# A planner's rule in a transformer block: LayerNorm of blocks 2 to 5 is taken first

## The chip, the cores and the metric

The kernel runs on one core of one Trainium2 chip. The core has a matrix engine (TensorE, PE in the profile), a vector engine (VectorE, DVE), an activation engine (ScalarE, ACT), a general engine (GpSimd, POOL) and a sequencer that issues transfers (SyncE, SP). Each engine executes its own stream of instructions in order and waits on semaphores for the others. The metric is the device time of one execution in microseconds (us).

## The reference

One transformer block on 2048 tokens of width 640, in float32. Attention has 32 heads of 20 columns and a sliding window of 256 keys; the feed-forward part is gated, 1536 wide.

```python
x = A_x                                               # [1, 2048, 640]
qkv = layernorm(x) @ wqkv                             # q, k, v: 32 heads of 20
scores = einsum("bhqd,bhkd->bhqk", q, k) * 20 ** -0.5
mask = (i - j >= 0) & (i - j < 256)                   # query i, key j
p = softmax(where(mask, scores, -1e9))
h = x + (p @ v) @ wo
g = layernorm(h)
out = h + (gelu(g @ w_gate) * (g @ w_up)) @ w_down
```

LayerNorm has no weights: (x - mean) / sqrt(var + 1e-5) over the 640 columns of a token.

## The kernel before, in words

The tokens are cut into 16 blocks of 128 (a block is one tile of 128 partitions), and two blocks make a chunk for the projections of q and k. A float32 product is made of three float16 products, so each operand is split into a high part and a low part: `xh`, `xl` for the normalised input, `w0h`, `w0l` (q), `w1h`, `w1l` (k), `w2h`, `w2l` (v), `w3h`, `w3l` (output projection) for the weights. ScalarE makes a high part, and VectorE makes the low part with one SCALAR_TENSOR_TENSOR of 128x640 (method `low`, L442).

The way of a block through the first half is this. `load_x` (L713) fetches it. `x_lane` (L673) runs `layernorm` (L467): two BN_STATS and one BN_AGGR on VectorE, an addition there, a power on GpSimd (tile `ly` with the lane's letter: `lyxc` for block 2, `lyxd` for block 3, `lyx` for block 4 and later), three small operations on VectorE, and one TENSOR_SCALAR of 128x640 that writes the normalised block in place (`pt` for blocks 1 to 3, `xt` for the others). Blocks 0 to 3 are then transposed on TensorE (`transpose_part`, L522): ScalarE copies the high part out, VectorE subtracts for the low part. Blocks 4 and later are split first (tile `xp`) and transposed by two DMAs on SP's queue (`turned`, L505). Then `qk` (L721) multiplies a chunk into bank `mm` on TensorE, in three groups of two, two and one tile of columns. `qk_out` (L746) takes a group out in tile `qks` (ScalarE the high part, VectorE the low part) and ScalarE's queue writes it to memory, from where `stack` (L767) fetches it back as `qT` and `kT` with six DMAs each on SP's queue. `vproj` makes v of a block in 30 matmuls.

Attention needs each row's maximum ahead of the exponentials. `maxima` (L833) multiplies q and k in bank `ra` or `rb` (matmuls `<-kT,qT`, 60 rows), and `max_out` (L905) reduces them on VectorE into `mxs` (CUSTOM_DVE into `junk`, then a read of the accumulator). When a block has all 32, `max_transpose` (L935) turns them on TensorE (tile `m`, then `mT`) and two DMAs of ScalarE's queue put them into two further rows of `qT`. `scores` (L950) multiplies again with these rows (matmuls `<-qT,kT`, 62 rows), ScalarE takes the exponential into `pt`, GpSimd masks it, and `value_lane` (L1015) multiplies with v into bank `pv`. The output projection and the whole feed-forward part follow; the first products of the latter fill TensorE while attention still runs.

What sets the order of all this is a planner inside the kernel. Class `Clock` (L54) keeps a modelled time for each engine. The program's pieces are generators ("lanes"), and each names the engine and the tiles that its next instruction needs. The main loop at the end of `block_kernel` goes through a list of lanes and lets the first that can start issue its next instruction; where none can, the modelled time goes on by 0.03 us. So a lane's place in the list and the lead that it is granted (variable `back`: how far ahead of the present its engine may already be planned) set the order of each engine's stream. Built once, the order is fixed. The list at L1636 is: lanes that must go soon, the list `early`, `outs` (results taken out of a bank: `qk_out`, `max_out`, the weights' `low`), `trans` (transposes), the other `sides`, and attention and dense products last. `early` holds every `x_lane` while the planner's condition at L1624 holds.

One more rule concerns TensorE. While no scores have been planned and TensorE has nothing to do by the plan, the loop issues a matmul that nothing reads, from the identity into bank `pv`; the text calls these fillers:

```python
if not pos["score"] and nc.t["tensor"] <= now:
    nc.tensor.matmul(pv[:, 0, :], ident16, ident16, start=True, stop=True)
```

They stand in TensorE's stream like any other matmul, and are executed there whether or not TensorE would have had to wait.

Of the kernel before, what the change touches and what calls it, by code (L numbers as in the profile page):

```python
# [253 lines left out]
def block_kernel(ctx: ExitStack, tc: tile.TileContext, x, wqkv, wo, wg, wu, wd, out):  # L254
# [44 lines left out]
    OUT, PREP, RAMPMAX, FFPREP, LATE = 0.75, 0.55, 0.25, 0.2, 0.4  # L299
    LEAD, TARGET = 20, 0.0  # L300
    XF = 1
    FFBACK = dict(split_lane=0.4, scale_lane=0.4, chunk_lane=0.3, token_sums=0.1,
                  sums_lane=0.2, norm_lane=0.2)
    EARLY = 0.6
# [234 lines left out]
    def products(n, term, ready=None, at_=None):  # L539


        ps = [at_[0]] if at_ else []
        col = at_[1] if at_ else 0

        def start(i):
            if ready and not ready(i) or not ps and opened["mm"] >= banks["mm"]:
                return INF
            t = nc.ready([x for ab in term(i) for x in ab], "tensor")
            return t if ps else max(t, nc.slot(psums["mm"], "mm", banks["mm"]))

        for i in range(n):
            yield ("tensor",), lambda i=i: start(i)
            if not ps:
                ps.append(bank("mm"))
            m = term(i)
            for k, (l, r) in enumerate(m):
                if k:
                    yield pe()
                o = ps[0][:, col:col + r.free_size()]
                nc.tensor.matmul(o, l, r, start=(i == 0 and k == 0),  # L560
                                 stop=(i == n - 1 and k == len(m) - 1))
                pos["dense"] += r.free_size() * 3 // len(m)
        return o
# [102 lines left out]
    B = [Block() for _ in range(NB)]  # L666
# [891 lines left out]
    class Lane:  # L1558
# [11 lines left out]
        def start(self, now):  # L1570

            if "tensor" in self.engs:
                return nc.t["tensor"] <= now + AHEAD and self.need() <= max(now, nc.t["tensor"])
            name = self.gen.__name__
            back = self.back
            if name in ("split_lane", "scale_lane"):
                back = PREP if not W["o", 0].ready else FFPREP
            elif name == "x_lane":
                back = EARLY if not B[XF].full else LATE
            elif name == "max_out" and not W["v"].ready:  # L1580
                back = RAMPMAX
            if isinstance(self.engs, Soon):
                back = max(back, OUT)
            if ffpools[1]:
                back = FFBACK.get(name, OUT)
            return (all(nc.t[e] <= now + back for e in self.engs if e != "sync")
                    and self.need() <= now + 0.1)
# [18 lines left out]
    sides, trans, outs = [], [], []  # L1606
# [7 lines left out]
    while dense.alive or sides or side or outs or tasks:  # L1614
        while side:
            back, gen = side.pop(0)
            sides.append(Lane(gen, back))
        while tps:
            trans.append(Lane(tps.pop(0), OUT))
        while tasks:  # L1620
            outs.append(Lane(tasks.pop(0), OUT))
        att_lanes = [rows, values]
        ahead = pos["dense"] / DENSE - pos["score"] / (H // 2) - TARGET
        early = [l for l in sides if l.gen.__name__ == "x_lane"] if not B[XF].full else []  # L1624
        if not W["v"].ready:
            att_first = maxq or nc.t["vector"] < nc.t["tensor"]
        else:
            att_first = ahead > 0
        if W["o", 0].ready:
            outs.sort(key=lambda l: l.gen.__name__ == "low")  # L1630
        if nc.mode == "row":
            early = [values] + early
        elif len(valq) < 2 and (maxq or scoreq):
            att_lanes = [rows]
        first = [l for l in [values] + trans + sides if isinstance(l.engs, Soon)]
        order = (first + early + outs + trans + sides  # L1636
                 + (att_lanes + [dense] if att_first else [dense] + att_lanes))
        for lane in order:
            if lane.alive and lane.start(now):
                break  # L1640
        else:
            if not pos["score"] and nc.t["tensor"] <= now:
                nc.tensor.matmul(pv[:, 0, :], ident16, ident16, start=True, stop=True)
            now += 0.03
            idle += 1
            assert idle < 20001, "nothing can be issued"
            continue
        idle = 0
        lane.step()
        trans = [l for l in trans if l.alive]  # L1650
        outs = [l for l in outs if l.alive]
        sides = [l for l in sides if l.alive]
# [44 lines left out]
```

## Time and profile before

| | us |
|---|---|
| median of 3 runs | 1022.67 (1022.4 to 1022.76) |
| the profiled execution, its own time | 1023.17 |
| its span, first to last instruction | 1021.3 |
| TensorE busy in the span | 999.8 |
| VectorE, ScalarE, GpSimd busy | 754.8, 437.0, 298.0 |

The profile comes from one execution, whose time is 0.5 us above the median; 1.9 us of it lie outside the span. In the rows of the timeline the first number is the start in us from the beginning of the span, the second the duration of the group, then engine, line, operation, output<-input, shapes and count; in brackets stands the idle time of the engine just ahead of it and who ended it. Almost all instructions are recorded under line L199, the line of a helper, so the tiles tell them apart. A matmul is shown with its whole passage through the array, so that rows of successive matmuls overlap: what one costs in a row of many is the distance between two starts.

### The profile page before, as it was taken

What the parts mean: (1) busy time and instruction counts of PE and PEld (TensorE: products, weight loads), DVE (VectorE), ACT (ScalarE), POOL (GpSimd) and SP (SyncE); (2) the same over time, 40 slices, a digit from 0 to 9 for tenths busy, and PEclk for the clock granted to TensorE, in tenths of its full rate; (3) what the DMA queues carried; (4) which work ended last, traced back from release to release, by engine and by line L of the source; (5) the groups of instructions that cost most, each with busy time, mean ns of one, the idle gap of its engine ahead of it and who ended that gap; (6) DMA issues with size and microseconds to landing.
All of it is one profiled execution on the core that took longest, in us unless ns stands there. A gap on an engine that the chain in (4) does not pass through costs nothing.

```text
span 1021.3 us, 30777 instructions
## 1 busy us (share of the span) xinstructions
PE 999.8 (98%) x12921; PEld 695.8 (68%) x12921; DVE 754.8 (74%) x2221; ACT 437.0 (43%) x706; POOL 298.0 (29%) x489
## 2 busy tenths in 40 slices
PE   8999999999999999999999999999999999999998
PEld 7875666676666676776655564567777777777776
DVE  6888998986787787474788788798996975544553
ACT  6514654656555564654558543522222222221220
POOL 7102223443343342342436321255313310000000
PEclk9999999999999999999999999999999999999999
DMA  8657667361551524225033433223553532222211
GB/s 306 137 116 175 184 145 168 81 163 55 91 122 44 114 57 118 42 61 127 3 131 106 92 117 103 78 104 127 161 177 90 161 138 78 78 96 86 78 53 52
DMA packets 105835, 112.67 MB, mean 110 GB/s; under 512 B 38369, under 2 KB 79585, under 8 KB 105697
## 3 DMA queue, kind: packets, MB, share of 16 engines
q1 hardware_dynamic: 93600, 99.97, 35.9%
q10 hardware_dynamic: 12096, 10.75, 3.4%
q8 instruction: 101, 1.65, 0.7%
q14 instruction: 38, 0.30, 0.1%
HBM read 73.73 MB, written 28.84 MB: 100 GB/s over the span
## 4 chain that ended last, share of the span: by engine, by line
PE 82%; DVE 8%; DMA 4%; ACT 2%; issue 2%; SPq 1%; POOL 0%; ACTq 0%; DVEq 0%
PE mm L199 41%; PE pv L199 12%; PE ra L199 11%; PE rb L199 10%; PE tp L199 7%; DVE junk L199 2%; DVE am L199 1%; DVE ht L199 1%; DMA v<-in_wqkv_dram 1%; DMA gu<-in_wqkv_dram 1%; SPq L199 1%; DMA qT<-mT 1%; DVE m L199 1%; ACT pt L199 1%; DMA h_dram<-ht 1%
## 5 line engine op out<-in xcount | busy, mean ns | idle before, releaser
L199 POOL TENSOR_SCALAR_AFFINE_SELECT pt<-pt 128x512 f32<-128x512 f32 x352 | 175.3, 513 | 278.2 <-ACT pt L199 262.6
L199 DVE CUSTOM_DVE_ANT_0 junk<-rb,band 128x320 bf16<-128x320 f32 x230 | 112.5, 489 | 41.3 <-PE rb L199 35.9
L199 DVE CUSTOM_DVE_ANT_0 junk<-ra,band 128x320 bf16<-128x320 f32 x218 | 106.6, 489 | 43.8 <-PE ra L199 38.3
L199 ACT ACTIVATE pt<-ra,esc 128x640 f32<-128x640 f32 (+2 forms) x131 | 99.6, 767 | 66.2 <-PE ra L199 53.3
L199 ACT ACTIVATE pt<-rb,esc 128x640 f32<-128x640 f32 (+2 forms) x125 | 94.9, 766 | 77.2 <-PE rb L199 56.5
L199 PE MATMUL pv<-pt,v 128*21 128x128 f32 x2880 | 104.1, 275 | 1.1 <-ACT oT L199 1.1
L199 PEld LDWEIGHTS <-ah 128*128 128x128 f16 x768 | 75.0, 98 | 29.5 <-issue 2.1
L199 ACT ACTIVATE gel<-gel,ffk 128x512 f32<-128x512 f32 x36 | 26.0, 721 | 138.0 <-DVE gel L199 138.0
L199 PEld LDWEIGHTS pv<-pt,v 128*21 128x21 f32 x2880 | 68.6, 100 | 11.9 <-issue 2.1
L199 PEld LDWEIGHTS <-ws 128*128 128x128 f16 x720 | 70.3, 98 | 8.3
L199 PEld LDWEIGHTS <-kT 62*64 62x64 f16 x2880 | 61.9, 107 | 13.9 <-issue 10.1
L199 PEld LDWEIGHTS <-qT 60*64 60x64 f16 x1280 | 29.8, 104 | 60.3 <-issue 51.3
L199 PEld LDWEIGHTS <-gu 128*128 128x128 f16 x440 | 42.1, 98 | 36.1 <-issue 2.5
L199 DVE SCALAR_TENSOR_TENSOR ht<-mm,ffk,ht 128x320 f32<-128x320 f32 x96 | 52.1, 545 | 10.9 <-PE mm L199 9.0
L199 ACT CAST ah<-gel 128x512 f16<-128x512 f32 x48 | 29.6, 617 | 64.4 <-DVE gel L199 64.2
L199 PE MATMUL mm<-xh,w1h 128*128 128x256 f16 x200 | 54.7, 274 | 1.3 <-DVE qks L199 1.3
L199 PE MATMUL mm<-xl,w1h 128*128 128x256 f16 x200 | 54.7, 273 | 0.0
L199 PE MATMUL mm<-xh,w1l 128*128 128x256 f16 x200 | 54.7, 273 | 0.0
L199 PE MATMUL mm<-w3l,oh 128*128 128x320 f16 x160 | 48.1, 301 | 0.1
L199 PE MATMUL mm<-w2h,xh 128*128 128x320 f16 x160 | 48.1, 300 | 0.0
L199 PE MATMUL mm<-w2h,xl 128*128 128x320 f16 x160 | 48.1, 301 | 0.0
L199 PE MATMUL mm<-w3h,ol 128*128 128x320 f16 x160 | 48.1, 300 | 0.0
(299 smaller groups left out, 2521.3 us busy)
## 6 DMA issues: line engine op xcount, KB each, us to landing
ws<-wsums SPq DMA_DIRECT2D x24, 640.0 KB
qk<-qks ACTq DMA_DIRECT2D x32, 256.0 KB
qT<-qk SPq DMA_DIRECT2D x48, 160.0 KB
kT<-qk SPq DMA_DIRECT2D x48, 160.0 KB
wsums<-ws SPq DMA_DIRECT2D x12, 640.0 KB
ht<-in_x_dram SPq DMA_DIRECT2D x16, 320.0 KB
h_dram<-ht SPq DMA_DIRECT2D x16, 320.0 KB
ht<-h_dram SPq DMA_DIRECT2D x16, 320.0 KB
```

The source lines that it names most:

```text
L199: r = real(*args, **kw)
```

## The change

Two expressions of the planner change. The list `early` holds the `x_lane`s until block 5 is ready and no longer only until block 1 is full, and in that time an `x_lane` may be planned 0.8 us ahead on its engine and no longer 0.4 us. No instruction of the computation is added or removed.

```diff
@@ Lane.start
             elif name == "x_lane":
-                back = EARLY if not B[XF].full else LATE
+                back = EARLY if not B[XF].full else 0.8 if not B[5].ready else LATE
@@ main loop
-        early = [l for l in sides if l.gen.__name__ == "x_lane"] if not B[XF].full else []
+        early = [l for l in sides if l.gen.__name__ == "x_lane"] if not B[5].ready else []
```

Every engine's stream is planned anew from there on. On VectorE, while the low parts of k's and q's weights are made (`w1l`, `w0l`), one piece of the difference of the two orders reads so (`lyxc`, `lyaxc` and `pt<-pt,lmvxc` belong to block 2, names with `xd` to block 3):

```order
+L199 SCALAR_TENSOR_TENSOR w1l<-gu,sw,w1h 128x640
 L199 TENSOR_TENSOR lyxc<-lyxc,lyaxc 128x1
 L199 TENSOR_SCALAR lvexd<-lmvxd 128x1
+L199 SCALAR_TENSOR_TENSOR qks<-mm,qs,qks 128x2x256
+L199 TENSOR_SCALAR pt<-pt,lmvxc,lyxc 128x640
+L199 SCALAR_TENSOR_TENSOR w1l<-gu,sw,w1h 128x640
+L199 SCALAR_TENSOR_TENSOR lyaxd<-lyxd,lvexd 128x1
+L199 SCALAR_TENSOR_TENSOR qks<-mm,qs,qks 128x256
 L199 SCALAR_TENSOR_TENSOR w0l<-qT,sw,w0h 128x640
-L199 SCALAR_TENSOR_TENSOR qks<-mm,qks 128x2x256
-L199 TENSOR_SCALAR pt<-pt,lmvxc,lyxc 128x640
```

The normalised block 2 now stands ahead of the last low part of k's weights and of all five of q's; before it stood behind them. The second group of the first q product (`qks<-mm,qs,qks 128x2x256`) has five more small instructions of LayerNorm ahead of it than before.

On SP's queue, where the first chunk's q and k are fetched back, the two orders differ so (`xh<-xp`, `xl<-xp` are the transposes of block 4, then of block 5; `qk_326`, `qk_423` and `qk_427` belong to the first chunk, the others to the second):

```order
 L199 DMA qT<-qk_326 20x16x256 x6
 L199 DMA xt<-in_x_dram 128x640
-L199 DMA kT<-qk_423 20x16x256 x6
 L199 DMA_TRANSPOSE xh<-xp 128x5x128
 L199 DMA_TRANSPOSE xl<-xp 128x5x128
 L199 DMA xt<-in_x_dram 128x640
-L199 DMA qT<-qk_863 20x16x256 x6
-L199 DMA kT<-qk_1059 20x16x256 x6
-L199 DMA wsl<-in_wo_dram 128x640
-L199 DMA ht<-in_x_dram 128x640
-L199 DMA wsl<-in_wo_dram 128x640
+L199 DMA kT<-qk_427 20x16x256 x6
```

The six transfers of the first `kT` now stand behind block 4's two transposes and a load.

On TensorE the dense products change places: of the second and third chunk's q and k more stands ahead of the first scores, of v less. Where the first product with v is made, the stream before had the next maxima right behind it:

```order
L199 MATMUL rb<-qT,kT 64x128
L199 MATMUL pv<-pt,v_119 21x128 x4
L199 LDWEIGHTS qT
L199 MATMUL rb<-kT,qT 64x320
L199 LDWEIGHTS qT
```

and has now nine matmuls of the v projection there, of which these are the first three:

```order
L199 MATMUL rb<-kT,qT 64x320
L199 MATMUL pv<-pt,v_119 21x128 x4
L199 LDWEIGHTS xl
L199 MATMUL mm<-w2h,xl 128x320
L199 LDWEIGHTS xh
L199 MATMUL mm<-w2h,xh 128x320
L199 LDWEIGHTS xh
L199 MATMUL mm<-w2l,xh 128x320
```

Counted over the whole program, TensorE's two streams hold the same matmuls but for the fillers: 324 before and 373 now. Of these, 277 stood ahead of the first maxima and 47 behind; now it is 238 and 135. From the transposition of block 13's maxima on (`tp<-ident,m`, at 472.07 us of the profile before) the two streams are the same row for row, but for which of the two banks `ra` and `rb` a row names.

## The prediction

> **What bounds the kernel now.** I read the page's first lines and its chain, then the table by stretches, then TensorE's timeline where the change acts, and last the engines that TensorE waits for there.
>
> ```profile
> PE 999.8 (98%) x12921; PEld 695.8 (68%) x12921; DVE 754.8 (74%) x2221; ACT 437.0 (43%) x706; POOL 298.0 (29%) x489
> PE 82%; DVE 8%; DMA 4%; ACT 2%; issue 2%; SPq 1%; POOL 0%; ACTq 0%; DVEq 0%
> L199 PE MATMUL pv<-ident 128*128 128x128 f16 x324 | 22.2, 228 | 2.5 <-DVE pv L199 2.5
> 23.65:51.70 28.05, 27.16 (x328) 24.36 (x326) 22.75 (x56) 15.66 (x31) 3.05 (x8) 1.00 0.64 128
> 51.70:90.00 38.30, 38.30 (x419) 26.73 (x418) 32.88 (x155) 7.24 (x16) 0.00 (x0) 1.00 0.54 124
> 90.00:135.00 45.00, 41.39 (x669) 27.56 (x669) 40.96 (x140) 27.55 (x53) 11.98 (x19) 1.00 0.73 179
> 135.00:200.00 65.00, 62.68 (x1062) 43.64 (x1059) 58.84 (x208) 38.88 (x64) 23.65 (x46) 1.00 0.55 139
> 200.00:300.00 100.00, 97.24 (x1979) 68.50 (x1978) 79.64 (x295) 55.21 (x86) 39.75 (x81) 1.00 0.52 108
> 300.00:472.00 172.00, 171.61 (x3282) 120.71 (x3280) 122.38 (x454) 91.29 (x141) 63.45 (x133) 1.00 0.32 77
> ```
>
> TensorE is busy 98% of the span and makes 82% of the chain. In the stretches (length, then busy us of PE, PEld, DVE, ACT, POOL, then the granted clock, 1.00 throughout) it idles 0.9, 0.0, 3.6, 2.3, 2.8 and 0.4 us. "Busy" there includes the fillers, the 324 matmuls of the third row, which compute nothing. So the time is TensorE's useful work, plus fillers, plus waits. The change leaves the useful work alone, and from 472 us on the two streams are the same; I take that part as unchanged. What is left to forecast is fillers and waits ahead of it.
>
> VectorE is the second bound: 91% busy from 90 to 135 and 91% from 135 to 200 us.
>
> **The change part by part.** These rows of the timeline carry the terms:
>
> ```profile
> 23.65 1.45 PE L199 MATMUL pv<-ident 128*128 128x128 f16 x23
> 25.99 0.27 PE L199 MATMUL mm<-xh,w1h 128*128 128x256 f16 x1 [0.89 <-DVE qks L199]
> 26.10 0.27 PE L199 MATMUL mm<-xl,w1h 128*128 128x256 f16 x1
> 35.09 0.39 PE L199 MATMUL ra<-ident,am 128*128 128x128 f32 x2
> 36.77 5.97 PE L199 MATMUL pv<-ident 128*128 128x128 f16 x104
> 42.58 0.30 PE L199 MATMUL mm<-w2h,xh 128*128 128x320 f16 x1
> 42.72 0.30 PE L199 MATMUL mm<-w2l,xh 128*128 128x320 f16 x1
> 51.70 0.43 PE L199 MATMUL ra<-kT,qT 60*64 60x128 f16 x8
> 90.03 0.31 PE L199 MATMUL ra<-qT,kT 62*64 62x128 f16 x8
> 93.25 0.33 PE L199 MATMUL rb<-kT,qT 60*64 60x320 f16 x4 [0.59 <-ACT pt L199]
> 95.03 0.33 PE L199 MATMUL ra<-kT,qT 60*64 60x320 f16 x4 [0.23 <-ACT pt L199]
> 99.03 0.33 PE L199 MATMUL rb<-kT,qT 60*64 60x320 f16 x4 [0.74 <-DVE mxs L199]
> 99.83 0.42 PE L199 MATMUL pv<-pt,v 128*21 128x128 f32 x8 [0.26 <-ACT oT L199]
> 107.56 0.64 PE L199 MATMUL pv<-pt,v 128*21 128x128 f32 x16 [0.45 <-ACT oT L199]
> 126.14 0.24 PE L199 MATMUL tp<-ident,m 128*64 128x128 f16 x1
> 133.45 0.33 PE L199 MATMUL rb<-qT,kT 62*64 62x128 f16 x11 [1.07 <-DMA qT<-mT]
> ```
>
> *Fillers.* The stream has 373 in place of 324. The row at 36.77 prices one: 104 of them run to the next row at 42.58, (42.58 - 36.77) / 104 = 0.056 us. The 49 more cost 49 x 0.056 = +2.7 us. Nothing hides them, since the stream executes them in order. Where they only replace a wait, that shows as a smaller wait in the terms below.
>
> *What is pulled forward.* Ahead of the first scores (90.03 in the row) there now stand 74 more matmuls of k, 75 more of q, 82 fewer of v and 28 more of the maxima. A q or k matmul is 0.11 us (25.99 to 26.10), a v matmul 0.14 (42.58 to 42.72), so that is 149 x 0.11 - 82 x 0.14 = +5 us, and the maxima are seven groups of four at about 0.3 (93.25 has 0.33), 2 us. The first scores come about 10 us later (5 + 2 + 2.7), but 7 of these are work that is missing behind; only the fillers remain. The first maxima move from 51.70 to about 57: 106 more of q and k ahead (+11.7), 30 fewer of v (-4.2), 39 fewer fillers (-2.2). VectorE sat idle ahead of them:
>
> ```profile
> 25.20 0.74 DVE L199 SCALAR_TENSOR_TENSOR qks<-mm,qs,qks 128x512 f16<-128x512 f32 x1
> 27.84 0.20 DVE L199 SCALAR_TENSOR_TENSOR lyaxc<-lyxc,lvexc 128x1 f32<-128x1 f32 x1
> 32.02 0.60 DVE L199 TENSOR_SCALAR pt<-pt,lmvxc,lyxc 128x640 f32<-128x640 f32 x1
> 52.18 0.29 DVE L199 CUSTOM_DVE_ANT_0 junk<-ra,mask 128x128 bf16<-128x128 f32 x1 [3.74 <-PE ra L199]
> 52.52 0.29 DVE L199 CUSTOM_DVE_ANT_0 junk<-ra,mask 128x128 bf16<-128x128 f32 x1
> 86.93 0.49 DVE L199 CUSTOM_DVE_ANT_0 junk<-ra,band 128x320 bf16<-128x320 f32 x1 [1.51 <-PE ra L199]
> 87.46 0.49 DVE L199 CUSTOM_DVE_ANT_0 junk<-ra,band 128x320 bf16<-128x320 f32 x1
> ```
>
> *New waits in the ramp.* The first k product waited until 25.99 for bank `mm`, which the qks row at 25.20 frees. Five small instructions of LayerNorm now stand ahead of that row, each about 0.1 (27.84 to the next start is 0.13), together 0.5 us; seven more fillers (0.4, counted above) run meanwhile, so +0.1 remains. ScalarE takes block 2's and 3's casts (rows below, 34.16 and 34.62, 0.46 apart) ahead of the last read of v's weights, whose maxima the matmul of 35.09 needs. That matmul had no wait; the casts bring it one of about 0.5, between 0 and 1.2 (both casts and 0.2 of queue). In the first eight groups of 128-wide maxima TensorE's pace is near VectorE's: 32 reductions at 0.34 (52.18 to 52.52) and two qks at 0.6 to 0.7 are 12 us of VectorE against 11 us of TensorE (85 fillers, 15 matmuls of k, 15 of v, eight groups at 0.33), with two banks between them: +0.3, from 0 to 0.9. Together +0.9, from 0 to 2.2.
>
> *Waits that go.* Once scores start, TensorE waits at 93.25, 95.03, 99.03, 99.83 and 107.56, in all 2.3 us. There the stream had no dense product between groups; now 5 to 10 matmuls of v lie between (0.7 to 1.4 us each time), more than the longest of these waits. The three waits for a bank (1.6) are likeliest to go, the two for `oT` stay, and I leave 0.4 for new ones: -1.2, from -2.3 to 0.
>
> *Maxima on their way.* From 126.14 block 2's maxima took a transposition, a copy and a DMA until the scores at 133.45, with 1.07 of waiting. Now 15 us of other work lies between, so that wait goes. Block 5 has only some 5.6 us there, worked out from the order with the prices above, against 7.3 here: it may wait up to 1.7, and I take 0.9. Net -0.2, from -1.1 to +1.0.
>
> *SP's queue.* The first `kT` stands behind two transposes:
>
> ```profile
> 34.16 0.58 ACT L199 CAST xh<-tp 128x512 f16<-128x512 f32 x1
> 34.62 0.60 ACT L199 CAST xh<-rb 128x512 f16<-128x512 f32 x1
> 41.80 4.82 SPq L199 DMA_DIRECT2D kT<-qk  x6
> 46.73 1.47 SPq L199 DMA_TRANSPOSE xh<-xp  x1
> 48.30 1.46 SPq L199 DMA_TRANSPOSE xl<-xp  x1
> 20.07 2.83 DVE L199 SCALAR_TENSOR_TENSOR w1l<-gu,sw,w1h 128x640 f16<-128x640 f32 x2 [0.39 <-ACT w1h L199]
> 23.62 1.66 DVE L199 SCALAR_TENSOR_TENSOR w1l<-gu,sw,w1h 128x640 f16<-128x640 f32 x2
> 18.82 3.39 POOL L199 TENSOR_TENSOR xl<-gu,xh 128x640 f16<-128x640 f32 x2
> ```
>
> Its issue moves from 41.80 by two transposes and a load, about 3.5 us, so it ends near 50 in place of 46.6. The first maxima, near 57 by TensorE's own order, cover that with about 7 us; before they had 5. Cost nothing; if the cover fails, TensorE waits at its first maxima and VectorE behind it.
>
> The rest of the waits up to 472 us (5.5 us from 135 on, by the stretches) belongs to the same work in a shifted order: 0, give or take 1.5.
>
> Sum: 2.7 + 0.9 - 1.2 - 0.2 = +2.2 us. The profiled execution took 1023.17, so a like one would take 1025.4; against the median of the runs, 0.5 lower, 1024.9.
>
> [...] Two low parts took 2.83 us beside GpSimd's additions and 1.66 without, so each addition (3.39 / 2 = 1.7 long) cost VectorE about 0.6. The second addition is now behind a power for block 2 and starts about 1 us later, against the same low parts: by the row, no change.
>
> [...]
>
> **The rivals.**
>
> *The waits pay for the fillers: no change.* All five waits of the score start go (-2.3), block 2's goes and no other comes (-1.1), and the ramp adds only 0.3. Then 2.7 + 0.3 - 3.4 = -0.4: 1022.3. For it speaks that v matmuls stand between the groups now; against it that ScalarE and VectorE are no faster.
>
> *VectorE's head start: faster.* At the first scores the new order has put 14 more reductions of 320 (0.53 each, 86.93 to 87.46), one LayerNorm with its split (2.6) and six qks (3.1) ahead, some 13 us of VectorE against 10 us of delay, mostly from the idle 3.74 and 1.51. If TensorE's waits from 90 to 200 us (3.6 + 2.3) are VectorE's lateness, they go as a whole: 2.7 + 0.5 - 5.9 = -2.7, 1020.0. It decides once more than 4.8 us of waits vanish. Against it: of these waits only the 0.74 names the maxima's reduction.
>
> *The start of attention comes late: clearly slower.* If the first `kT` or block 5's transposes land after TensorE has reached them, each us is lost on both engines. The transposes stand 3.5 us ahead of `kT`; a queue later by half of that beyond the cover, with the upper end of the ramp's waits, gives 2.7 + 2.2 + 1.8 - 1.2 = +5.5: 1028.2.
>
> **How the numbers follow.** Forecast (+1 to +4, so 1023.7 to 1026.7) 0.45; no change 0.25; head start 0.15; late attention 0.15. About 0.2%, or 2.05 us, is what runs of this kernel can tell from no change. Of the forecast's 0.45 some four fifths lie above that, with late attention 0.51 slower; the other fifth and the no-change case make 0.34 the same; 0.15 faster. The range runs from 1020.8, which takes in half of the head start, to 1028.5.
>
> **What would show it.** Right: 373 fillers; the first maxima of TensorE near 57 us and the first scores near 100; VectorE idle ahead of the first maxima still 3 to 5 us; waits on `pt` and `mxs` shortly behind the first scores smaller than 1.6 us in sum; the transposition of block 13's maxima 2 to 3 us after 472.07, and the same distance to the end behind it. Wrong: that row at or ahead of 472, or a wait of over 1 us at the first maxima on `kT`, or a changed distance from it to the end.

## The result and the profile after

The changed kernel takes 1028.32 us (median of 8 runs, 1026.92 to 1030.42). The kernel before took 1022.84 us in its runs beside it. The ratio is 1.0052 with a 95% interval of 1.0038 to 1.0066, which is 3.9 to 6.8 us slower. In a second set of runs (below) the same kernel stood 0.58% above before. The forecast was 1024.9, slower, with a range to 1028.5: right in sign, and about 3 us too small; the measured time lies 0.2 us inside the upper end of the range.

The page's first lines, its chain, the row of the fillers, and then the table by stretches, of the kernel after (columns as in the prediction):

```profile
PE 1004.5 (98%) x12970; PEld 701.6 (68%) x12970; DVE 755.5 (73%) x2221; ACT 436.9 (42%) x706; POOL 299.4 (29%) x489
PE 82%; DVE 6%; DMA 5%; ACT 4%; issue 2%; SPq 1%; POOL 1%; ACTq 0%; DVEq 0%
L199 PE MATMUL pv<-ident 128*128 128x128 f16 x373 | 26.1, 229 | 2.5 <-DVE pv L199 2.5
...
51.70:90.00 38.30, 37.24 (x477) 28.23 (x475) 29.74 (x148) 5.41 (x11) 0.55 (x1) 1.00 0.67 129
90.00:135.00 45.00, 43.25 (x621) 28.62 (x621) 39.02 (x130) 25.98 (x54) 12.68 (x16) 1.00 0.53 143
135.00:200.00 65.00, 62.82 (x1084) 42.55 (x1086) 58.79 (x210) 37.47 (x62) 24.22 (x45) 0.97 0.63 154
200.00:300.00 100.00, 97.04 (x1919) 68.72 (x1912) 80.61 (x294) 54.29 (x87) 37.79 (x78) 1.00 0.50 105
300.00:472.00 172.00, 170.27 (x3352) 119.75 (x3351) 123.85 (x462) 94.84 (x144) 65.86 (x139) 1.00 0.33 75
```

The 373 fillers are there. The wait of 90 to 135 us shrank from 3.6 to 1.8 us, as forecast. Three things are new: TensorE idles 1.1 us from 51.7 to 90 us, where it idled 0.0; the granted clock is 0.97 from 135 to 200 us; and TensorE idles 1.7 us from 300 to 472, where it idled 0.4.

TensorE's timeline of the kernel after, the rows that answer to those of the prediction and some of the longest waits behind them:

```profile
25.92 0.27 PE L199 MATMUL mm<-xh,w1h 128*128 128x256 f16 x1 [0.49 <-DVE qks L199]
34.86 0.46 PE L199 MATMUL ra<-ident,am 128*128 128x128 f32 x2
56.61 0.24 PE L199 MATMUL ra<-kT,qT 60*64 60x128 f16 x1
57.91 0.30 PE L199 MATMUL ra<-kT,qT 60*64 60x128 f16 x7 [1.06 <-issue]
101.12 0.31 PE L199 MATMUL rb<-qT,kT 62*64 62x128 f16 x8
102.37 0.31 PE L199 MATMUL rb<-qT,kT 62*64 62x128 f16 x8 [0.49 <-ACT pt L199]
105.76 0.30 PE L199 MATMUL mm<-w2h,xh 128*128 128x320 f16 x1 [0.94 <-DVE qks L199]
168.41 0.22 PE L199 MATMUL tp<-ident,m 128*64 128x128 f16 x1 [1.53 <-DVE h0l L199]
170.31 0.41 PE L199 MATMUL ra<-kT,qT 60*64 60x320 f16 x3 [0.25 <-DMA kT<-qk]
241.55 0.25 PE L199 MATMUL rb<-kT,qT 60*64 60x64 f16 x3 [1.63 <-DMA kT<-qk]
480.93 0.86 PE L199 MATMUL pv<-pt,v 128*21 128x128 f32 x24
489.51 0.33 PE L199 MATMUL ra<-kT,qT 60*64 60x320 f16 x3 [1.54 <-DMA kT<-qk]
550.43 0.24 PE L199 MATMUL tp<-ident,m 128*64 128x128 f16 x1 [0.85 <-DVE m L199]
```

Of the kernel before, the rows that stand against four of these:

```profile
166.34 0.33 PE L199 MATMUL rb<-kT,qT 60*64 60x320 f16 x3 [1.28 <-issue]
232.66 0.25 PE L199 MATMUL ra<-kT,qT 60*64 60x64 f16 x3 [0.82 <-DMA kT<-qk]
476.56 0.85 PE L199 MATMUL pv<-pt,v 128*21 128x128 f32 x24
544.28 0.24 PE L199 MATMUL tp<-ident,m 128*64 128x128 f16 x1 [0.85 <-DVE m L199]
```

The product with v at 476.56 is at 480.93 now, 4.4 us later. The last transposition of maxima (block 15's, 544.28) is at 550.43, 6.1 us later, and the span ends 7.1 us later. This profiled execution took 1030.42, which is 2.1 above the median of its runs, so not all of the 7.1 belongs to the change.

**A sum that holds for every kernel of this study.** All of them have the same useful matmuls ahead of block 15's transposition, so the start of that row should be one constant, plus fillers (0.056 us each), plus the bracketed waits of TensorE from 24 us on, plus what a low clock takes (the missing part of the granted clock, in windows of 5 us, times 5). I worked this out for 14 profiles, those of all runs below among them, from TensorE's whole timeline. What is left over is 515.5 us on average with a standard deviation of 1.2 (513.1 to 518.1), so these three items explain the differences to about 1 us, in single profiles to 2.6:

| profile | fillers | waits | clock | left over | start of the row |
|---|---|---|---|---|---|
| before | 18.1 | 10.2 | 0 | 516.0 | 544.3 |
| before, second profile | 18.1 | 10.3 | 3.4 | 514.6 | 546.4 |
| after | 20.9 | 12.3 | 1.7 | 515.6 | 550.4 |
| after, second profile | 20.9 | 10.9 | 3.5 | 514.0 | 549.3 |

### The profile page after: what moved, and what is told of

Same layout as the page of the kernel before. It is cut to its first block, busy times and chain, and to the rows that moved or that the text cites. A ratio compares the mean times of both kernels' runs of the same rounds, so it can differ in the third digit from the quotient of the medians.

```text
span 1028.4 us, 30873 instructions
## 1 busy us (share of the span) xinstructions
PE 1004.5 (98%) x12970; PEld 701.6 (68%) x12970; DVE 755.5 (73%) x2221; ACT 436.9 (42%) x706; POOL 299.4 (29%) x489
## 4 chain that ended last, share of the span: by engine, by line
PE 82%; DVE 6%; DMA 5%; ACT 4%; issue 2%; SPq 1%; POOL 1%; ACTq 0%; DVEq 0%
PE mm L199 41%; PE pv L199 13%; PE ra L199 12%; PE rb L199 10%; PE tp L199 7%; DMA kT<-qk 3%; ACT pt L199 1%; DVE junk L199 1%; SPq L199 1%; DVE am L199 1%; DMA xl<-xp 1%; DVE ht L199 1%; DMA wst<-in_wu_dram 1%; DMA h1h<-wsl 0%; ACT wst L199 0%
## 5 line engine op out<-in xcount | busy, mean ns | idle before, releaser
L199 POOL TENSOR_SCALAR_AFFINE_SELECT pt<-pt 128x512 f32<-128x512 f32 x352 | 177.6, 519 | 322.3 <-ACT pt L199 307.6
L199 DVE CUSTOM_DVE_ANT_0 junk<-ra,band 128x320 bf16<-128x320 f32 x228 | 111.4, 489 | 43.7 <-PE ra L199 38.0
L199 DVE CUSTOM_DVE_ANT_0 junk<-rb,band 128x320 bf16<-128x320 f32 x220 | 107.5, 489 | 33.6 <-PE rb L199 28.4
L199 ACT ACTIVATE pt<-rb,esc 128x640 f32<-128x640 f32 (+2 forms) x130 | 99.4, 771 | 74.7 <-PE rb L199 63.2
L199 ACT ACTIVATE pt<-ra,esc 128x640 f32<-128x640 f32 (+2 forms) x126 | 95.4, 764 | 66.2 <-PE ra L199 51.8
L199 DVE SCALAR_TENSOR_TENSOR ht<-mm,ffk,ht 128x320 f32<-128x320 f32 x96 | 52.1, 544 | 10.9 <-PE mm L199 9.0
L199 PE MATMUL mm<-w3h,oh 128*128 128x320 f16 x160 | 48.2, 301 | 1.3 <-DVE qks L199 0.6
```

The source lines that it names most:

```text
L199: r = real(*args, **kw)
```

## The experiments

The theory on trial (F) was that of the prediction: fillers are paid in full. The rivals were that VectorE sets the pace anyway (V), and that the fillers keep up the granted clock (C). Two further theories came up with the first results: K, keys that wait on SP, and W, a weight load that comes late.

Each run also gives its mean granted clock to 0.001. Over all 207 runs, a straight line with a level of its own for each set of runs (13 of other runs, and all shared runs of before as one) gives 1.07 (standard error 0.10) us for each 0.001 of clock that is missing; single runs scatter 1.7 us around it. "At equal clock" below is a kernel's level at a clock of 1, with its standard error, over that of before (1021.7 us). A mean of 0.999 thus costs 1 us, of 0.996 4 us. The figure is only as good as the one slope for all kernels: where no run of a kernel reached a clock of 1, it is carried past what was measured. A profile shows one execution, which need not lie near the median of its kernel; where it is over 2 us away from it, the text says so.

The edits are shown shortened: counters, and the call `plan`, which counts an instruction's time in the planner without issuing it, are left out of those that move a transfer.

**Fillers out of before.**

```diff
-nc.tensor.matmul(pv[:, 0, :], ident16, ident16, start=True, stop=True)
+if pos["max"]:        # planned, not issued
+    nc.tensor.plan("matmul", pv[:, 0, :], [ident16[:], ident16[:]])
+else:
+    nc.tensor.matmul(pv[:, 0, :], ident16, ident16, start=True, stop=True)
```

> The kernel before, without the 47 filler matmuls (identity times identity, result unused) that it issues behind the first maxima; their planned time is still counted, so every other instruction keeps its order. Nothing of the result is left out. Theory F (fillers are paid in full, because TensorE's stream sets the end): 47 x 0.056 us = 2.6 us less, about 1020.2 us, ratio 0.997. Rival V (VectorE sets the pace between 58 and 100 us, so TensorE only waits where a filler stood): the same time as before, within 1 us. Rival C (fillers hold the granted clock up through the gaps): the clock of some windows before 110 us falls below 1 and the time rises by 1 us or more.

Measured: 1025.97, ratio 1.0036 (1.0017 to 1.0055): slower. At equal clock it is 0.4 +- 0.6 us above before, so the 2.6 us did not come back, and the mean clock fell from 0.999 to 0.996. Windows of this kernel where scores start (columns as above, the granted clock is the third from the end):

```profile
90.00:95.00 5.00, 2.91 (x56) 1.60 (x48) 2.95 (x14) 2.74 (x7) 2.37 (x4) 0.97 1.10 257
95.00:100.00 5.00, 5.00 (x58) 2.60 (x50) 4.21 (x17) 3.61 (x7) 1.38 (x2) 0.50 0.65 202
```

TensorE is busy 2.9 of 5 us, and then runs at half the clock. The waits up to block 15's transposition add to 13.3 us in place of 10.2: what the fillers took became waits. F fails for fillers taken out; V and C both act.

**Fillers doubled in before.**

```diff
+if pos["max"]:        # second one, unplanned
+    nc.tensor.real.matmul(pv[:, 0, :], ident16, ident16, start=True, stop=True)
```

> The kernel before, with the 47 filler matmuls behind the first maxima each issued twice, the second one without planned time, so every other instruction keeps its order. Theory F (paid in full): 47 x 0.056 = +2.6 us, about 1025.4 us, ratio 1.0026. Rival V (hidden under VectorE's work on maxima): within 1 us of before. With both this kernel and the one without fillers, F wants a straight line through before: -2.6, 0, +2.6.

Measured: 1026.14, ratio 1.0033 (1.0016 to 1.0051); at equal clock +2.9 +- 0.5 us. Added fillers are paid in full, as F says. The straight line through all three kernels isn't there: fillers added cost their price, fillers removed give nothing.

**Fillers out of after.** The same edit in the kernel after, 135 fillers.

> The kernel after, without the 135 filler matmuls that it issues behind the first maxima, order of everything else kept. Theory F: 135 x 0.056 = 7.6 us less than the kernel after (1028.3), so 1020.7 us, and 0.5 us above the kernel before without its own 47 if fillers are most of the change's cost; if this kernel stays 2 to 3 us above that one, the rest of the loss lies in the later order (the wait for the transposed keys at 489.5 us and the wait with the clock's fall at 168 us). Rival V: within 1 us of the kernel after, since in this stage VectorE's LayerNorms are what is waited for. Rival C: the granted clock falls in 58 to 100 us and less than half of the 7.6 us comes back.

Measured: 1027.31, ratio 1.0038 (1.0021 to 1.0055), 12 runs from 1022.69 to 1029.84. At equal clock it is 0.6 +- 0.6 above before, where after itself stands 5.5 +- 0.6 and, in its second set of runs, 3.8 +- 0.7 above: 3 to 5 us of the 7.6 come back, and then the clock (0.996) takes 3 of them. TensorE and then the windows of 1 us, this kernel:

```profile
68.42 0.50 PE L199 MATMUL ra<-kT,qT 60*64 60x256 f16 x8 [1.30 <-DVE mxs L199]
```

```profile
67.00:68.00 1.00, 0.12 (x8) 0.00 (x0) 0.77 (x6) 0.00 (x0) 0.00 (x0) 1.00 0.00 0
68.00:69.00 1.00, 0.58 (x9) 0.28 (x10) 0.82 (x7) 0.00 (x0) 0.00 (x0) 0.81 0.45 137
69.00:70.00 1.00, 1.00 (x5) 0.55 (x4) 0.93 (x7) 0.00 (x0) 0.00 (x0) 0.50 0.60 157
```

With the fillers gone one sees what they stood on: TensorE waits for VectorE's reduction of a group of maxima, three times over 1 us from 65 to 69 us. This profile is that of the fastest of the 12 runs (1022.69), so its waits may be fewer than in most.

The expectation named a second test, this kernel against before without its late fillers. At equal clock the two stand 0.3 +- 0.7 us apart, and both have a mean clock of 0.996. A loss of 2 to 3 us in the later order, past the fillers, does not show between them. So at equal clock the cost of the change goes when the late fillers go; that it is simply their price is contradicted by the next run.

**Half of after's fillers.** Every second one behind the first maxima is not issued (68 of 135).

> The kernel after, with every second of its fillers behind the first maxima left out (68 of 135), order of the rest kept. Theory C (fillers cost time at full clock but hold the granted clock): without any, time at equal clock fell by 4.8 us, but the clock fell from 0.999 to 0.996, which took 3.2 us back. With half, the clock should stand between, and the time is at or under the middle, 1027 us or less; if the clock stays at 0.999, some 1025 us. If the fall of the clock has nothing to do with fillers, the clock stays 0.999 or is as low as 0.996 with no order in it.

Measured: 1028.78, ratio 1.0063 (1.0047 to 1.0080); at equal clock +5.0 +- 0.7, the same as after. The clock held (0.998), but most of the 3.8 us are found as waits again (14.7 us of waits against 12.3 and 10.9 in the two profiles of after). From 24 to 112 us they add to 4.6 us, against 3.0 and 1.7 there. A wait of 3.23 us at 170.00 for the residual `h0l` says nothing of the fillers: the unchanged kernel has 1.5 or 4.0 at that place. The forecast of 1027 or less missed.

**The lead alone.** Only `back = ... 0.8 ...` of the change. The other edit alone leaves all five orders as they were (so it was not run): with a lead of 0.4 us the longer list `early` changes nothing.

> The kernel before, with one of the two edits alone: the lead of 0.8 us for LayerNorm of blocks 2 to 5 in the planner's comparison, but the old condition on the list that lets these blocks go ahead of all other sides. (The other edit alone leaves the order of all five engines as it was, so it is not run.) It has 37 fillers more than before, where both edits together have 49. If the lead does the whole change: 37 x 0.056 = +2.1 us of fillers and the same waits and later order as after, +4 to +5 us, 1027 us. If the loss past the fillers is an accident of the order that the two edits together fall into: +2.1 us, 1025 us, with no wait of over 1 us for transposed keys between 476 and 500 us.

Measured: 1027.56, ratio 1.0046 (1.0027 to 1.0064). At equal clock +2.1 +- 0.6, which is what its 37 more fillers cost (2.1); the rest is its clock, 0.996, and no wait for keys of over 1 us stands from 476 to 500 us. That is the second expectation at equal clock, though the time came out like the first. So the lead alone moves the order and costs nearly as much time as the whole change, but more of it through the clock.

**Blocks 2 and 3 only.** Both edits with `B[3].ready` in place of `B[5].ready`.

> The kernel before with both edits, but only for blocks 2 and 3 (ready condition on block 3 in place of block 5). It issues 344 fillers, 20 more than before, where after has 49 more. If the cost at equal clock is that of the fillers, plus nothing else that follows from the blocks: 20 x 0.056 = +1.1 us at a clock of 1. If the two early LayerNorms themselves delay the stream: over +2 us already.

Measured: 1027.47 (5 runs), ratio 1.0056 (1.0042 to 1.0071). The mean clock is the lowest of all, 0.994, and at equal clock the kernel is no slower than before (-0.3 +- 0.9). Windows at the start of its scores:

```profile
95.00:100.00 5.00, 2.51 (x60) 1.48 (x63) 3.90 (x15) 3.40 (x9) 2.57 (x5) 0.93 0.84 231
100.00:105.00 5.00, 5.00 (x60) 2.82 (x59) 4.28 (x18) 3.46 (x8) 2.42 (x4) 0.50 0.16 62
```

Here half the change costs as much as the whole, and by the common slope almost all through the clock; its five runs lie between 0.993 and 0.995, so the level at a clock of 1 is carried far. Neither of my two expectations had that.

**The kernel after, unchanged.**

> The kernel after once more, unchanged, beside the same runs of before as the next three. If its cost is fixed in the program: 5.3 us over before again, and the waits of 1.5 us at 168 us (a transposition behind a late weight load) and at 489.5 us (transposed keys) show again. If these two waits are accidents of one execution: they are shorter or stand elsewhere, and the granted clock of the ramp differs. From the runs so far, time rises by 1.05 us for each 0.001 of mean granted clock that is missing, and at a clock of 1 the kernel after stands 5.4 +- 0.7 us above before.

Measured: 1027.58, ratio 1.0058 (1.0043 to 1.0073). The cost came again; single waits did not. At 489.5 us there was none this time, and the one at 168 us was 4.01. TensorE, then VectorE, then windows, of this execution:

```profile
170.82 0.27 PE L199 MATMUL tp<-ident,m 128*64 128x128 f16 x1 [4.01 <-DVE h0l L199]
```

```profile
169.16 0.69 DVE L199 TENSOR_REDUCE am<-wsl 128x1 f32<-128x512 f32 x1 [4.61 <-DMA wsl<-in_wu_dram]
...
170.09 0.68 DVE L199 TENSOR_TENSOR h0l<-tp,h0h 128x512 f16<-128x512 f32 x1
```

```profile
165.00:170.00 5.00, 1.63 (x39) 1.09 (x39) 0.84 (x2) 2.72 (x6) 1.42 (x3) 0.81 0.86 172
170.00:175.00 5.00, 4.18 (x41) 2.10 (x40) 3.21 (x9) 0.51 (x2) 1.75 (x3) 0.50 0.54 149
```

VectorE stands at a reduction of an MLP weight slice whose load is late, `h0l` stands behind it, and TensorE behind that.

**Keys past the store at 475 us.** The store of a block to `h_dram` and the next load of `ht`, which stood among the six `kT` transfers on SP's queue, go to ScalarE's.

```diff
-nc.sync.dma_start(h_dram[j * P:(j + 1) * P, :], b.h)
+if pos["kt7"]:        # while the last chunk's keys are fetched
+    nc.scalar.real.dma_start(h_dram[j * P:(j + 1) * P, :], b.h)
```

> The kernel after, with two transfers of block rows (a store of a finished block and a load of the next) taken out of SP's queue, where they stand among the last six transfers of transposed keys, and issued on ScalarE's queue; the six then stand together. Theory K (the keys wait on SP behind the store, which waits for VectorE): the wait of 1.54 us at 489.5 us goes, the time is 1.5 us under the kernel after. Rival: ScalarE, which now waits for VectorE ahead of the store with its copies of values behind it, gives it back: no change or up to 2 us more.

Measured: 1027.85, ratio 1.0064 (1.0049 to 1.0079); at equal clock +5.2 +- 0.7, no gain. The wait for keys isn't there, but the unchanged kernel lacked it too in its second profile, so this does not show that the move removed it. In its place stands a wait for ScalarE, as the rival had it; ScalarE itself waits for the moved store. TensorE, then ScalarE:

```profile
482.06 0.34 PE L199 MATMUL ra<-qT,kT 62*64 62x128 f16 x12 [1.39 <-ACT pt L199]
```

```profile
481.22 0.79 ACT L199 ACTIVATE pt<-ra,esc 128x640 f32<-128x640 f32 x1 [3.10 <-DMA h_dram<-ht]
```

**Weight loads past the keys, in after.** Three of the loads that SP issues behind `kT` go to ScalarE's queue; in a second kernel only the one that VectorE waits for. TensorE's and VectorE's orders stay.

```diff
-nc.sync.dma_start(t, self.src[:, i, :])
+if self.col == C_G and pos["ld", C_G] > 8 or self.col == C_U and pos["ld", C_U] == 1:
+    nc.scalar.real.dma_start(t, self.src[:, i, :])
+else:
+    nc.sync.dma_start(t, self.src[:, i, :])
```

> The kernel after, with three of the loads of MLP weights (gate slices 9 and 10, up slice 1; SP issues them at 159.7 to 161.6 us, right behind three transfers of keys that hold SP from 152.3 to 159.6 us) issued on ScalarE's queue; nothing else moves on TensorE or VectorE. Theory W (from 164 us VectorE's reduction of the up slice waits 2.1 to 4.6 us for this load, the residual behind it comes late, and TensorE's transposition at 168 us waits 1.5 to 4.0 us; the granted clock falls to 0.5 to 0.66 right behind): the wait falls under 1 us, the window 165 to 175 us keeps its clock, and the time falls by 2 to 4 us, to 1024 to 1026 us. If the load is late because of its own transfer and not of SP's queue, or ScalarE loses by the issues: the same time as after within 1 us.

> The kernel after, with one load alone (up slice 1, the one that VectorE's reduction waits for from 164 us) issued on ScalarE's queue: the counterpart of the one load moved in the kernel before, which made that kernel 2.7 us faster. Theory W with the load alone: TensorE's wait at 168 us shrinks from 1.5 to 4.0 us to under 1 us and the time falls to 1025 to 1026 us. Theory K2 (the keys of the next chunk land near 170 us whatever this load does, as when three loads were moved: a wait of 2.78 us for keys stood at 170.15 us): the residual's wait goes and a wait for keys of 1 us or more stands within 3 us behind it, and the time stays within 1 us of the kernel after.

Measured: 1029.00, ratio 1.0073 (1.0052 to 1.0094), and 1026.88, ratio 1.0045 (1.0023 to 1.0067); at equal clock +4.7 +- 0.7 and +5.2 +- 0.5, neither a gain. With three loads moved VectorE's reduction had its data at once and TensorE's wait for `h0l` was gone, but the next one came 2 us on, for the write of q and k that the keys are fetched from; with one load moved it came for the keys. That second profile is of a slow execution (1032.22, 5.3 above the median of its runs). VectorE with three, TensorE with three, then TensorE with one:

```profile
163.52 0.68 DVE L199 TENSOR_REDUCE am<-wsl 128x1 f32<-128x512 f32 x1
```

```profile
170.15 0.33 PE L199 MATMUL ra<-kT,qT 60*64 60x320 f16 x3 [2.78 <-DMA qk<-qks]
```

```profile
169.68 0.33 PE L199 MATMUL ra<-kT,qT 60*64 60x320 f16 x3 [2.62 <-DMA kT<-qk]
```

W falls for the kernel after, and K2 (the keys land near 170 us whatever the load does) holds. The chain of waits of the first profiles fits that. Of the kernels before and after, the piece that covers this place:

```profile
163.12 3.57 DMA wsl<-in_wu_dram
```

```profile
162.83 7.44 DMA kT<-qk
```

Before, the chain runs through the weight load; after, through the keys, and the residual's wait at 168 us is one beside it. But the second profiles of the same two kernels say otherwise. Before's chain names no weight load there, and after's does:

```profile
167.72 1.87 issue
```

```profile
162.10 7.03 DMA wsl<-in_wu_dram
```

So the chain of one execution does not decide it; the runs with the loads moved do.

**The weight load past the keys, in before.** Here the chain of the first profile names the load, so the same kind of edit was made there: `if self.col == C_U and pos["ld", C_U] == 4`, one transfer on ScalarE's queue, nothing else moved.

> The kernel before, with one load of MLP weights (up slice 4, which SP issues at 163.1 us behind three transfers of keys that hold SP from 154.5 us, and for which VectorE's reduction waits 3.3 us until 166.7 us) issued on ScalarE's queue. Theory W: the load lands some 2.5 us sooner, TensorE's waits at 163.5 to 168.1 us (0.47 + 1.28 + 0.46 us) shrink by 1.3 us or more, and fewer runs have a clock under 1; 1020.5 to 1021.5 us, faster than both kernels. If the load is not what TensorE waits for: no change.

Measured: 1020.34, ratio 0.9974 (0.9959 to 0.9988), faster than before and after. At equal clock it is 1.5 +- 0.5 below before, and its clock is 0.9998 where before has 0.9988, which is the other 1 us. TensorE and VectorE of this kernel:

```profile
166.62 0.33 PE L199 MATMUL rb<-kT,qT 60*64 60x320 f16 x3 [0.67 <-DMA wsl<-in_wu_dram]
```

```profile
166.79 0.69 DVE L199 TENSOR_REDUCE am<-wsl 128x1 f32<-128x512 f32 x1 [2.52 <-DMA wsl<-in_wu_dram]
```

TensorE's waits at this place shrank from 2.2 (0.47, 1.28 and 0.46) to 1.2 us (0.25, 0.67 and 0.26). The expectation that the load lands 2.5 us sooner failed: VectorE still waited 2.5 us where it waited 3.3. This profile is that of the slowest of the 12 runs (1023.20, 2.9 above their median), so it can't show how the time was gained; the gain stands, its mechanism is argued.

**The kernel before, unchanged.**

> The kernel before once more, unchanged, for a second profile beside the same runs. No difference to before is expected. If the profiled run has a mean clock of 0.998 (as 15 of the 35 runs of before in the first comparison had), the window in which the clock falls lies at 165 to 175 us, behind the wait for the weight load that the kernel before has too (3.3 us on VectorE).

Measured: 1024.78, ratio 1.0012 (0.9994 to 1.0030), no difference. Its profiled run had two falls of the clock, the second where expected. TensorE:

```profile
135.33 0.33 PE L199 MATMUL rb<-qT,kT 62*64 62x128 f16 x11 [1.96 <-DMA qT<-mT]
169.59 0.33 PE L199 MATMUL rb<-kT,qT 60*64 60x320 f16 x3 [1.87 <-issue]
```

## Why the prediction was right in sign and too small

The model (useful work, fillers, waits) held; it lacked the clock, which was 1.00 in every stretch of the one profile that I had. The clock is not what parts the two kernels, though: both have a mean of 0.998 to 0.999 over their runs. At equal clock after stands 5.5 +- 0.6 and 3.8 +- 0.7 us above before, about 4.8 together. The terms, as forecast and as the profiles have them (fillers as count times price; waits as means over after's two profiles and the one with keys moved, less means over before's two):

| term | forecast, us | found, us |
|---|---|---|
| fillers | +2.7 | +2.7 |
| new waits in the ramp (24 to 90 us) | +0.9 | -0.3 |
| waits that go at the score start (90 to 112) | -1.2 | -0.9 |
| maxima on their way (112 to 140) | -0.2 | -1.3 |
| rest of the waits (140 to 483) | 0, +-1.5 | +3.1 |
| behind that, to block 15's transposition | 0 | +0.6 |
| sum | +2.2 | +4.0 |

*Fillers.* Number and price were right, and doubling them confirmed the price. "Nothing hides them" was only half right: taken out, they leave waits (3.1 us of 2.6 in before, 3 of 3.8 with half of after's; with all 135 out, 3 to 5 us of 7.6 came back at equal clock, and the clock then took 3). They are issued where TensorE has nothing to do by the plan, and VectorE's reductions are what it waited for there in the kernel without them (1.30 us at 68.42). So none of these runs saved time by leaving them out, and how much of the 4.8 us is theirs stays open.

*Waits in the ramp.* The first maxima came at 56.61 (forecast 57), VectorE idled 3.65 us ahead of them (forecast 3 to 5; 2.12 in the second profile), the first scores came at 101 (forecast 100). But the first k product waited less than before (0.49 against 0.89), and the matmul of the weights' maxima at 34.86 did not wait at all, where I had put 0.5. A wait of 1.06 at 57.91, for which the profile names no releaser, stood in one profile and not in the next.

*Waits that go.* The score start waits 1.5 us in place of 2.3 on the mean, on `pt` and `qks`; that on `mxs` is gone.

*Maxima on their way.* Block 2's wait on `qT<-mT` (1.07 and 1.96 us in before's two profiles) is gone, and block 5's, for which I had put 0.9, did not come. That is 1.1 us better than forecast.

*SP's queue.* `kT` was issued until 50.2 us (forecast: near 50) and delayed nothing. Its cost of zero was right there.

*The rest of the waits up to 472 us, 0 give or take 1.5.* This is the step that failed: measured +3.1. From 140 to 483 us TensorE waits 6.7, 7.7 and 7.4 us in the three profiles of after, 5.1 and 3.2 in before's two. Of this, 1.1 us stands from 140 to 200 us (2.0, 4.9 and 2.9 against 2.2 and 2.1), where single waits for the residual `h0l` go up to 4.0. The other 2.0 us stand behind 200 us. About 1.0 of it is the wait for keys at 241 us, which stands in every profile of the order after (1.3 to 1.6 us). Before has 0.8 and 0.4 at its like, but its versions with an edit have from under 0.3 to 1.7, so the order before is not free of it. Another 0.6 is a wait for `qks` at 238 us. Others at 300, 360 or 489 us come and go. I had taken "the same work in a shifted order" for neutral. Before's order had 0.3 us of waits from 300 to 483, so shifting it could mostly lose there, and the term should have had a positive middle. Why the keys and loads come later against TensorE was not tested apart, and the profiles are few. With the edited kernels taken in, the waits from 140 to 483 are 3.1 to 7.3 us in five profiles of the order before and 5.4 to 10.5 in seven of the order after. The two kernels without late fillers have 7.3 (before) and 5.4 (after), the other way round.

*Luck in the sum.* The term that failed is 3.1 us off, and the two terms for waits that were to come in the ramp or behind block 2 are 1.2 and 1.1 us off the other way. That the sum is under 2 us off is in part because these cancel.

*From 472 us on unchanged.* Nearly: 0.6 us more wait to block 15's transposition on the mean. Behind it the two kernels have 477.0 and 477.2 against 478.0 and 477.6 us to the end.

*GpSimd beside VectorE.* From the rows I had taken 0.6 us of VectorE's time for each of GpSimd's additions, and no change from the later start of the second one. VectorE and then GpSimd, after:

```profile
20.01 1.68 DVE L199 SCALAR_TENSOR_TENSOR w1l<-gu,sw,w1h 128x640 f16<-128x640 f32 x2 [0.39 <-ACT w1h L199]
22.01 0.95 DVE L199 SCALAR_TENSOR_TENSOR lyaxc<-lyxc,lvexc 128x1 f32<-128x1 f32 x1
```

```profile
20.17 1.13 POOL L199 TENSOR_TENSOR lyxc<-lvexc,mhalf 128x1 f32<-128x1 f32 x1
21.27 1.68 POOL L199 TENSOR_TENSOR xl<-gu,xh 128x640 f16<-128x640 f32 x1
```

The two low parts ran beside the power (1.13 us) and were not held up: 1.68 us, where before they took 2.83 beside the additions and two others took 1.66 without. What met the addition was a VectorE instruction of 128x1 elements. It took 0.95 us, where before it took 0.20 (at 27.84), and ended with the addition (22.96 and 22.95). Why that one was late the rows do not show, and GpSimd's spans are rough. The first k product, at 25.92, did not feel it: it came at 25.99 before.

One statement ahead of the prediction was inexact: the transposition of block 13's maxima is not yet a row at which the streams agree, since a product of the output projection stands ahead of it before and behind it now. It is at 473.31 after, which would read as +1.2; the first row that can be compared is the product with v, 476.56 and 480.93. The sign that I named there was thus a wrong mark.

Of the rivals, "the waits pay for the fillers" got the score start right and missed the late waits. "Head start" failed: VectorE's earlier LayerNorm shortened TensorE's waits by about 1 us and not 5.9. "Late attention" gave nearly the time measured, by luck: its keys and transposes were in time at the start, where it had them late, and waits grew from 140 us on. What stays open: about 1 us between the sum (4.0) and the runs (4.8 +- 0.5), which is within their errors; which of the late waits an execution draws; and how the cost divides between late fillers and later order, on which the sum and the two kernels without late fillers disagree.

## What to carry to other kernels

Where one engine's stream sets the end, count what stands in it, what it waits and at what clock it runs, and compare versions at equal clock; a term for "the same work in another order" is not zero when the old order had hardly any waits. Idle-time fillers are paid when added (47 more of them: +2.9 +- 0.5 us at equal clock), but one that stands where the engine would wait gives little or nothing when removed (47 fewer: +0.4 +- 0.6 us), and may be what holds the clock (a mean of 0.999 with them, 0.996 without). Of two waits at one place the chain of a single profile can name either: the same kind of edit gained 0.26% in one kernel and nothing in the other, and two profiles of the other named different transfers. Move the transfer and time it over many runs.

## What was not expected of the hardware

The granted clock of this single core falls to half (0.50), for about 3.4 us or twice that, shortly behind a wait or within one. In windows of 1 us of the kernel after, behind its wait of 1.53 us that ended at 168.41:

```profile
170.00:171.00 1.00, 0.75 (x12) 0.22 (x14) 0.24 (x1) 0.00 (x0) 0.00 (x0) 0.71 0.92 285
171.00:172.00 1.00, 1.00 (x24) 0.79 (x24) 0.82 (x5) 0.00 (x0) 0.00 (x0) 0.50 0.78 280
172.00:173.00 1.00, 1.00 (x11) 0.36 (x3) 0.94 (x4) 0.15 (x1) 0.00 (x0) 0.50 0.06 23
173.00:174.00 1.00, 1.00 (x18) 0.43 (x20) 0.48 (x2) 0.11 (x1) 0.00 (x0) 0.58 0.33 36
```

The missing parts are 0.29 + 0.50 + 0.50 + 0.42 = 1.7 us, all lost where TensorE is the bound; at half the clock that makes a fall of 1.7 / 0.5 = 3.4 us. In three profiles (after's second, before without its late fillers, blocks 2 and 3 only) the missing parts of one fall add to 3.4 us, so it lasted 6.8. Falls came behind single waits of 1.46 us (after with one load moved, at 300.51) and more, within one of 4.0 us (after's second profile: 0.56 from 168 to 169 us, while TensorE waited until 170.82), and behind several short ones with TensorE busy half the time (blocks 2 and 3 only, 2.51 of 5 us). Others had none: 1.6 us (after, at 241.55, clock 1.00 from 240 to 250) and 2.6 us (after with one load moved, at 169.68, clock 1.00 from 165 to 175). So the length of one wait does not decide whether the clock falls, and no run here shows what does.
